# A fused local, downsampled and mixture-of-experts kernel: attention products as 64-row tiles, two heads at once in two PSUM banks

## The chip, the cores and the metric

The kernel runs on one core of a Trainium2 chip. The metric is the device time of one execution in microseconds. Before the change three runs gave 767.11, 763.87 and 763.42 us, so the median is 763.87 us.

## The reference

The inputs q, k and v have 8 batches, 8 heads, 576 positions and 64 elements per head, all fp32. Two attentions are added, and the sum is the token matrix of a mixture of experts.

```python
q_d = q.reshape(B, H, S // 4, 4, D).mean(axis=3)      # k_d, v_d likewise
out_d = sm_attn(q_d, k_d, v_d)                        # 144 x 144 per head
out_up = np.repeat(out_d, 4, axis=2)
mask = np.abs(pos[:, None] - pos[None, :]) < 4        # a band of 7 keys
out_local = softmax(where(mask, q @ k.T / 8, -1e9)) @ v
x = (out_up + out_local) as 4608 tokens of 512
logits = x @ w_gate                                   # 8 experts, 576 tokens each
# tokens and experts are paired greedily by falling logit
out[mask_e] = relu(x[mask_e] @ w1[e]) @ w2[e]
```

## The kernel before, in words

The program has two stages. The first computes the attention, the logits and, while it ends, the first steps of the routing. The second ranks the logits and runs the experts, one after the other, with gathers and scatters of tokens. The change touches the first stage alone.

**Units.** The local attention is cut into windows of 32 queries (QW), 18 of them to a batch; a window needs at most 38 keys (KW). Four windows make a unit `u` of 128 tokens, so there are 36 units, four and a half to a batch. A unit passes the steps s0 and s1 (scores, four heads each), t (the transposed weights), v0 and v1 (products with v), add (the downsampled part is added), st (the token row is stored), lt and lm (transposes and logits).

**Transposed q and k.** `trw` makes Q^T and K^T from rows of the input: four 128x128 transposes on TensorE (PE) fill a PSUM bank, and two copies of 64 partitions by 512 elements take it to SBUF (`evac`, L276 on VectorE (DVE) and L278 on ScalarE (ACT)). There are eight such steps to a batch. `trt` does the last 64 positions by products with the identity matrix (L306). K^T holds two heads, one on partitions 0 to 63 and one on 64 to 127. Q^T is kept in `qz` with a plane for each of the two heads, in which the other head's 64 partitions are zeros, so that a product over all 128 partitions gives one head's scores.

**Local scores and values.** `loc_s` puts the mask into a bank by one product with the identity (L428) and adds 32 products of 32 queries by 38 keys (L436), on four column tiles of the array. DVE takes the maximum and subtracts it (L444, L445), ACT takes the exponential. `loc_t` transposes the weights (L454), and two ACT copies (L465) place them in `pt`, in which zeros separate two windows. `loc_v` does 16 products of 64 columns by 65 (L476); `vw` holds the keys of v of one unit, two windows one above the other on the partitions, with a column of ones for the denominators. `norm` divides (L404, L405, L407).

**Downsampled attention.** `gsum` adds groups of four columns of Q^T and K^T, mostly on GpSimd (POOL). `down_s` makes the scores of three heads in a bank (L325, and L328 for the last 16 positions); DVE reads each bank twice (L331, L333). `down_t` and `down_v` transpose and multiply, and the result goes to DRAM (`up_dram`), from where each unit reads its rows again (`up`).

**PSUM.** All steps of the stage rotate through the eight banks of one pool, `g`.

**Order.** `run` gives every step a time in units (a table of offsets: LOC, TW, DW, DWS, NEXT, LD0, LD1), sorts all steps by it and writes the instructions in that order, with no scheduler behind it. `after(n, f)` puts a step off by n pieces of PE work. All loads of the stage are issued by SyncE (SP) in the same sorted order: `nat` (rows of q, k, v by batch), `natt`, `natw`, and `vw` with four DMAs to a unit.

## Time and profile before

| what | value |
|---|---|
| median of three runs | 763.87 us |
| the profiled execution's own time | 763.21 us |
| its span, first to last instruction | 761.5 us |
| mean granted TensorE clock | 0.948 |
| busy share of the span: PE, DVE, ACT, POOL | 88%, 71%, 44%, 32% |
| weight loads (PEld) | 61% |
| moved by DMA | 126.43 MB, 166 GB/s over the span |
| packets of under 512 bytes | 97012 of 152980 |

The page gives every engine's busy time; the busy share over the whole span mixes the attention stage with the experts, so the stage has to be cut out first. A row of the grouped view names the line, the engine, the tile written and the tiles read, the shape, the number of instructions, their busy time together, the mean of one, and the idle time before them with what ended it. Products of fp32 show two records each, a transpose one. Records of different column tiles overlap in time, so their cost is read from the start of one group to the start of the next and not from the mean of one.

### The profile page before, as it was taken

The page shows a single profiled execution, that of the slowest core. Times are in us where ns is not written, and L with a number is a line of the kernel's source. Part 1 is how long each engine was busy: PE and PEld are TensorE (multiplying, and loading weights), DVE is VectorE, ACT ScalarE, POOL GpSimd, SP SyncE. Part 2 cuts the span into 40 slices and gives each one's busy share as a digit, 9 for nine tenths or more (in the row PEclk, how much of TensorE's full clock was granted, in tenths as well). Part 3 has the DMA queues.
Part 4 walks back from the last instruction along what each step waited for, and adds up shares of the span by engine and source line. Part 5 has one row for each costly group of instructions (what it writes and reads, how often), then busy time and mean ns, then how long its engine had stood idle before and what let it go on. Part 6 is the DMA issues. An engine that isn't in the chain of part 4 may idle for free.

```text
span 761.5 us, 21142 instructions
## 1 busy us (share of the span) xinstructions
PE 673.8 (88%) x8545; PEld 467.4 (61%) x8545; DVE 537.3 (71%) x1614; ACT 333.5 (44%) x646; POOL 245.8 (32%) x282
## 2 busy tenths in 40 slices
PE   7789898898889893399899999999999999999994
PEld 5667676787768772276366457466467475674851
DVE  5977879598786986887879889889888154261200
ACT  3437676475757541341436234326224253342210
POOL 8173544447453751200530613130410402202011
PEclk8979999899999996589999999999999999999998
DMA  9978798998979861530935663684744933404001
GB/s 283 186 189 205 221 205 244 224 261 199 267 209 263 218 195 54 160 124 14 299 98 222 145 220 107 136 273 163 194 163 167 220 109 108 103 2 117 9 28 35
DMA packets 152980, 126.43 MB, mean 166 GB/s; under 512 B 97012, under 2 KB 127220, under 8 KB 152884
## 3 DMA queue, kind: packets, MB, share of 16 engines
q1 hardware_dynamic: 145424, 103.30, 50.7%
q0 software_dynamic: 6512, 21.24, 9.1%
q8 instruction: 68, 1.11, 0.6%
q10 hardware_dynamic: 948, 0.55, 0.3%
q14 instruction: 28, 0.23, 0.1%
HBM read 95.56 MB, written 21.23 MB: 153 GB/s over the span
## 4 chain that ended last, share of the span: by engine, by line
issue 29%; DVE 24%; PE 23%; DMA 12%; POOL 5%; ACT 4%; SPq 1%; POOLq 0%; DVEq 0%; ACTq 0%
PE pX L1139 5%; PE pH L1110 4%; POOL out_dram L1147 3%; DMA up<-up_dram 3%; DVE cmp L709 2%; DMA nat<-in_q_dram 2%; DMA up_dram<-xu 2%; DMA nat<-in_k_dram 2%; PE pR L743 2%; DVE wl L1050 2%; DMA xg<-x_dram,idx 2%; PE g L292 2%; DVE x L407 1%; POOL xg L1074 1%; PE g L476 1%
## 5 line engine op out<-in xcount | busy, mean ns | idle before, releaser
L1110 PE MATMUL pH<-xt,wh 128*128 128x256 f16 (+1 forms) x1024 | 194.2, 287 | 3.3 <-DVE ht L1126 2.5
L1139 PE MATMUL pX<-wh,ht 128*128 128x512 f16 (+1 forms) x640 | 181.3, 382 | 0.0
L1110 PE MATMUL pH<-xt,wl 128*128 128x320 f16 (+1 forms) x512 | 146.4, 286 | 0.0
L1147 POOL DMA_INDIRECT out_dram<-y,idx x40 | 47.8, 1195 | 282.1 <-ACT y L1144 263.1
L1139 PEld LDWEIGHTS <-ht 128*128 128x128 f16 (+1 forms) x960 | 81.1, 100 | 90.1 <-issue 5.6
L1139 PE MATMUL pX<-wl,ht 128*128 128x512 f16 (+1 forms) x320 | 118.9, 382 | 0.0
L1110 PEld LDWEIGHTS <-wh 128*128 128x128 f16 x1024 | 98.0, 98 | 30.7 <-DVE ht L1126 4.2
L1123 ACT ACTIVATE ht<-pH 128x512 f16<-128x512 f32 (+1 forms) x128 | 45.4, 407 | 102.5 <-PE pH L1110 102.4
L1050 DVE SCALAR_TENSOR_TENSOR wl<-nat,wh 128x512 f16<-128x512 f32 x128 | 84.6, 683 | 2.5
L1144 ACT ACTIVATE y<-pX 128x512 f32<-128x512 f32 (+1 forms) x40 | 23.8, 594 | 126.7 <-PE pX L1139 71.1
L1126 DVE SCALAR_TENSOR_TENSOR ht<-pH,ht 128x512 f16<-128x512 f32 (+1 forms) x128 | 52.4, 449 | 34.5 <-ACT ht L1123 34.2
L1074 POOL DMA_INDIRECT xg<-x_dram,idx x40 | 45.0, 1126 | 85.6 <-DVE idx L1001 66.5
L1048 ACT ACTIVATE wh<-nat 128x1024 f16<-128x1024 f32 x64 | 66.9, 1056 | 4.3 <-DMA nat<-in_moe_w_dram 4.2
L465 ACT COPY pt<-g 64x512 f32<-64x512 f32 x72 | 41.7, 579 | 38.0 <-PE g L454 36.8
L1110 PEld LDWEIGHTS <-wl 128*128 128x128 f16 x512 | 50.1, 98 | 12.4 <-issue 0.2
L1094 DVE SCALAR_TENSOR_TENSOR xs<-xg,xs 128x512 f16<-128x512 f32 (+1 forms) x35 | 23.2, 685 | 40.1 <-ACT xs L1093 40.1
L292 PE MATMUL g<-ident,nat 128*128 128x128 f32 x256 | 40.3, 293 | 11.0 <-DMA nat<-in_q_dram 3.6
L476 PE MATMUL g<-vw,pt 128*64 128x65 f32 x1152 | 44.1, 227 | 4.5 <-ACT pt L465 1.8
L476 PEld LDWEIGHTS g<-vw,pt 128*64 128x64 f32 x1152 | 39.1, 140 | 11.5 <-ACT pt L465 6.4
L278 ACT COPY kt<-g 64x512 f32<-64x512 f32 (+1 forms) x53 | 33.3, 629 | 26.0 <-PE g L292 12.0
L265 POOL TENSOR_TENSOR gtmp<-qz 64x576 f32<-64x576 f32 x28 | 32.0, 1142 | 34.0 <-DVE kdt L268 26.2
L499 DVE SCALAR_TENSOR_TENSOR xt<-g,xt 128x512 f16<-128x512 f32 x36 | 24.6, 685 | 21.2 <-ACT xt L498 21.1
(222 smaller groups left out, 1165.8 us busy)
## 6 DMA issues: line engine op xcount, KB each, us to landing
nat<-in_moe_w_dram SPq DMA_DIRECT2D x28, 1024.0 KB
vw<-in_v_dram SPq DMA_DIRECT2D x136, 96.0 KB
up<-up_dram SPq DMA_DIRECT2D x36, 256.0 KB
x_dram<-x SPq DMA_DIRECT2D x36, 256.0 KB
nat<-in_q_dram SPq DMA_DIRECT2D x16, 512.0 KB
nat<-in_k_dram SPq DMA_DIRECT2D x16, 512.0 KB
nat<-in_v_dram SPq DMA_DIRECT2D x14, 512.0 KB
up_dram<-xu SPq DMA_DIRECT2D x16, 128.0 KB
```

Of the source, the lines that this page charges most:

```text
L278: self.nc.scalar.copy(out, in_)
L292: nc.tensor.transpose(p[:, a, :, fp], src[:, 4 * hh + 2 * a + s, 2 * fp:2 * fp + 2].rearrange("p f d -> p (f d)"), self.ident)
L465: self.nc.scalar.copy(out, in_)
L476: nc.tensor.matmul(o[64 * i:64 * i + 64, 65 * h:65 * h + 65], pt[:, 2 * g + i, h].rearrange("p b q -> p (b q)"), self.vw[u % 4][:, i, 4 * ...
L1048: nc.scalar.activation(hi, r, AF.Copy, scale=sc)
L1050: nc.vector.scalar_tensor_tensor(lo[:, a:a + LOP], r[:, a:a + LOP], sc, hi[:, a:a + LOP], op0=OP.mult, op1=OP.subtract)
L1074: self.fetched = nc.gpsimd.indirect_dma_start(out=xg[:n], out_offset=None, in_=self.x, in_offset=bass.IndirectOffsetOnAxis(ap=idx[:n, c:c ...
L1110: mm = nc.tensor.matmul(p[:, s, :s1 - s0], w[d][a][:, 128 * f:128 * f + 128], xt[:, b, d, s0:s1], start=j == 0, stop=j == len(seq) - 1)
L1123: last = nc.scalar.activation(hi, q, AF.Relu)
L1126: nc.vector.scalar_tensor_tensor(lo, q, 0.0, hi, op0=OP.max, op1=OP.subtract)
L1139: nc.tensor.matmul(p[o:o + m], ht[:, f, h0:h0 + m], w[4 + f // 2][b][:, 512 * (f % 2):512 * (f % 2) + 512], start=j < parts, stop=j >= len ...
L1147: i = nc.gpsimd.indirect_dma_start(out=self.out, in_=y[:n], in_offset=None, out_offset=bass.IndirectOffsetOnAxis(ap=idx[:n, c:c + 1], axis=0))
```

## The change

Q^T has no zeros any more: like K^T it holds two heads on 128 partitions. Every product with it names a tile of 64 rows of the array, at row 0 or 64, and the two heads' products follow each other directly. They write two PSUM banks, which are allotted as a pair. The pool has four single banks `g` (NG) and two pairs `gg` (NG2) now; scores of both kinds and the local products with v use pairs, all else single banks.

`trw` makes both heads of a pair at once, by eight products with the identity of 128 rows by 64 columns (L286 in the new program) in place of four transposes, and one copy of 128 partitions by 512. `loc_s` does all eight heads in one step; `loc_t` needs one copy and no zeros; `loc_v` does 32 products of 64 rows by 32 columns in one step, and divides once. `down_s` does six heads in a pair, then two and the last positions. `vw` holds the keys of nine windows, half a sequence, in three buffers, and is loaded by 10 or 12 DMAs whose issue is spread by 0.1 unit. `EV` shares the copies of `evac` evenly between ACT and DVE, where one in five was DVE's; the offsets of the table are other numbers.

```diff
-EV = (0, 0, 0, 0, 1)
+EV = (1, 1, 0, 0)
+NG, NG2 = 4, 2
...
-LD0 = (-2.849, -3.627, -0.654, -0.8, 0.549)
+LD0 = (-2.934, -3.869, -0.654, -0.983, 0.549)
...
-            self.vw.append(cst.tile([128, 2, H, D + 1], F32, name=f"vw{i}"))
+            self.vw.append(cst.tile([128, 9, HP, D + 1], F32, name=f"vw{i}"))
...
+    def bank(self):
+        return self.ps.tile([128, 512], F32, name="g", bufs=NG)
+
+    def banks(self):
+        return self.ps.tile([128, 2, 512], F32, name="gg", bufs=NG2)
...
-    def trw(self, b, which, hh, s):
+    def trw(self, b, which, hp):
...
-        p = self.ps.tile([128, 2, GM, 2], F32, name="g", bufs=8)
-        for a in range(2):
-            for fp in range(2):
-                nc.tensor.transpose(p[:, a, :, fp], src[:, 4 * hh + 2 * a + s, 2 * fp:2 * fp + 2].rearrange("p f d -> p (f d)"),
-                                    self.ident)
...
-        for par in range(2):
-            self.evac(t[:, :, par:4 * GM:2], p[64 * par:64 * par + 64].rearrange("p a i f -> p a (i f)"), par)
+        p = self.bank().rearrange("p (i f) -> p i f", f=4)
+        for f in range(4):
+            for s in range(2):
+                nc.tensor.matmul(p[64 * s:64 * s + 64, :, f], src[:, 2 * hp + s, f], self.ident, start=True, stop=True)
+        self.evac(self.dest(b, which)[:, hp, :4 * GM], p.rearrange("p i f -> p (i f)"))
...
+        def score(o, hp, s):
             r = slice(64 * s, 64 * s + 64)
+            nc.tensor.matmul(o, q[r, hp, :GM], k[r, hp], start=True, stop=True, tile_position=(64 * s, 0))
...
-            for a in range(4):
-                h = 4 * g + a
-                nc.tensor.matmul(sv[32 * a:32 * a + 32, 4 * g + c], self.qz[b % 2][:, h // 2, h % 2, QW * w:QW * w + QW],
-                                 self.kt[b][:, h // 2, key0(w):key0(w) + KW], start=False, stop=True,
-                                 skip_group_check=True, tile_position=(0, 32 * a))
+        for a in range(HP):
+            for c in range(4):
+                b, w = divmod(4 * u + c, NW)
+                for s in range(2):
+                    r = slice(64 * s, 64 * s + 64)
+                    nc.tensor.matmul(o[32 * c:32 * c + 32, s, a], self.xt_["q", b][r, a, QW * w:QW * w + QW],
+                                     self.xt_["k", b][r, a, key0(w):key0(w) + KW], start=False, stop=True,
+                                     skip_group_check=True, tile_position=(64 * s, 32 * c))
...
-        for a in range(2):
-            r = slice(64 * a, 64 * a + 64)
-            self.pevac(a, out[r, :, :, a], p[r].rearrange("p (i h q) -> p i h q", h=4, q=QW))
+        nc.scalar.copy(self.pt[u].rearrange("p a q -> p (a q)"), p)
...
-        for h in range(4):
-            for i in range(2):
-                nc.tensor.matmul(o[64 * i:64 * i + 64, 65 * h:65 * h + 65],
-                                 pt[:, 2 * g + i, h].rearrange("p b q -> p (b q)"),
-                                 self.vw[u % 4][:, i, 4 * g + h], start=True, stop=True)
+        for a in range(HP):
+            for c in range(4):
+                j, i = divmod(4 * u + c, 9)
+                vw = self.vw[j % NVW]
+                for s in range(2):
+                    r = slice(64 * s, 64 * s + 64)
+                    nc.tensor.matmul(o[32 * c:32 * c + 32, s, a], pt[r, a, 32 * c:32 * c + 32], vw[r, i, a],
+                                     start=True, stop=True, tile_position=(64 * s, 32 * c))
```

Two places of the order matter for the prediction. The first is PE about the scores of the downsampled attention, in batch 2. Before, each bank is one of eight; L494 is lt, L476 v, L292 trw, L325 and L328 down_s, L428 and L436 the local scores, L454 t, L306 trt.

```order
L494 MATMUL g<-ident,x 128x128 x4
L476 MATMUL g<-vw_130,pt_134 64x65 x16
L292 MATMUL g<-ident,nat 128x128 x4
L325 MATMUL g<-kdt,qdz_120 128x144 x3
L428 LDWEIGHTS identb
L428 MATMUL g<-mask,identb 128x304
L436 MATMUL g<-kt,qz_119 32x38 x16
L454 MATMUL g<-ident,sw_131 128x128 x4
L436 MATMUL g<-kt,qz_119 32x38 x16
L292 MATMUL g<-ident,nat 128x128 x4
```

In the new program the same work stands like this, `gg` being a pair; L465 is v, L286 trw, L307 and L324 down_s, L426 and L434 the local scores, L450 t.

```order
L465 MATMUL gg<-vw_121,pt 32x65 x32
L286 MATMUL g<-ident,nat 64x128 x16
L307 MATMUL gg<-kdt,qdt 128x144 x6
L426 LDWEIGHTS identb
L426 MATMUL gg<-mask,identb 128x152
L426 LDWEIGHTS identb
L426 MATMUL gg<-mask,identb 128x152
L434 MATMUL gg<-kt,qt 32x38 x32
L450 MATMUL g<-ident,sw_125 128x128 x4
L307 MATMUL gg<-kdt,qdt 128x144 x2
L324 MATMUL gg<-kdt,qdt 32x144 x4
```

v, the first down_s, the local scores and the second down_s now each take one of the two pairs, in this order; t and trw take single banks. The local scores are one step and no longer two with t between them.

The second place is SP at the start, where v's keys are loaded. Before, the first eight `vw` DMAs (units 1 and 0) stand ahead of the last quarter of the next batch's q and k.

```order
L206 DMA natw_162<-in_v_dram 128x1x256
L215 DMA nat_164<-in_v_dram 128x8x256
L215 DMA nat_246<-in_q_dram 128x4x256
L215 DMA nat_248<-in_k_dram 128x4x256
L215 DMA nat_246<-in_q_dram 128x4x256
L229 DMA vw1_128<-in_v_dram 48x8x64 x4
L229 DMA vw0_127<-in_v_dram 48x8x64 x4
L215 DMA nat_248<-in_k_dram 128x4x256
L200 DMA natt_268<-in_q_dram 64x1x256 x2
```

In the new program the pieces of both halves of the sequence alternate; the end of that stretch, after seventeen of their DMAs, reads:

```order
L210 DMA vw1_122<-in_v_dram 48x8x64
L210 DMA vw0_121<-in_v_dram 48x8x64
L183 DMA natt_279<-in_q_dram 64x1x256 x2
L183 DMA natt_279<-in_k_dram 64x1x256 x2
L210 DMA vw1_122<-in_v_dram 48x8x64
L210 DMA vw0_121<-in_v_dram 48x8x64 x2
```

The last pieces of `vw0`, which the first unit's v needs, now stand behind the pieces of `vw1`, behind the whole of the next batch's first q and k and behind its `natt`.

More of the change, by code (lines that the diff above doesn't have):

```diff
@@ L318, in down_s @@
     def down_s(self, b, part):
         nc = self.nc
-        s = self.ps.tile([128, 512], F32, name="g", bufs=8)
-        sv = s[:, :3 * G].rearrange("p (c k) -> p c k", c=3)
-        for c in range(3):
-            hp, i = divmod(3 * part + c, 2)
-            if hp < HP:
-                nc.tensor.matmul(sv[:, c], self.qdz[b % 2][:, hp, i], self.kdt[b][:, hp], start=True, stop=True)
-        if part == 2:
+        q, k = self.xd["q", b], self.xd["k", b]
+        def score(o, hp, s):
+            r = slice(64 * s, 64 * s + 64)
+            nc.tensor.matmul(o, q[r, hp, :GM], k[r, hp], start=True, stop=True, tile_position=(64 * s, 0))
@@ new lines, in down_s @@
+        if part == 0:
+            n = 6
+            o = self.banks()[:, :, :3 * G].rearrange("p s (c k) -> p s c k", c=3)
+            for hp in range(3):
+                for s in range(2):
+                    score(o[:, s, hp], hp, s)
+            t = self.sd[:, :6]
+            tv = t.rearrange("p (c s) k -> p s c k", s=2)
+            todo = (o, tv, 6),
+        else:
+            n = 3
+            o = self.banks()[:, :, :2 * G].rearrange("p s (c k) -> p s c k", c=2)
+            for s in range(2):
+                score(o[:, s, 0], 3, s)
@@ L332, in down_s @@
-        t = self.sd[:, 3 * part:3 * part + 3]
-        nc.vector.tensor_tensor(t, sv, mx[:, :, None].to_broadcast([128, 3, G]), op=OP.subtract)
+            t = self.sd[:, 6:]
+            todo = (o[:, :, 0], t[:, :2], 2), (o[:, 0, 1:], t[:, 2:], 1)
+        for o, tv, m in todo:
+            mx = self.wk.tile([128, m], F32, name=f"mxd{m}")
+            mv = mx.rearrange("p (s c) -> p s c", s=2) if m == 6 else mx
+            nc.vector.tensor_reduce(mv, o, axis=AX.X, op=OP.max)
+            nc.vector.tensor_tensor(tv, o, mv[..., None].to_broadcast(list(o.shape)), op=OP.subtract)
@@ L417, in load_up, with loc_s @@
         self.up[u] = t
-    def loc_s(self, u, g):
+    def loc_s(self, u):
         nc = self.nc
-        if g == 0:
-            s = self.ps.tile([128, 512], F32, name="g", bufs=8)
-            self.so[u] = s
-            nc.tensor.matmul(s[:, :H * KW], self.identb, self.mask[:, None, ukind(u)].to_broadcast([128, 2, 4 * KW]),
+        o = self.banks()[:, :, :HP * KW]
+        for s in range(2):
+            nc.tensor.matmul(o[:, s], self.identb, self.mask[:, None, ukind(u)].to_broadcast([128, HP, KW]),
```

286 lines of the change are left out of this document (129 added, 157 removed).

## The prediction

> **What bounds the kernel now.** I cut the span into stages first, with the busy time of each engine by stretch. The columns are the stretch, its length, then busy time and instructions of PE, weight loads, DVE, ACT and POOL, the granted clock, the busy share of the DMA engines and GB/s.
>
> ```profile
> 0.00:27.00 27.00, 17.95 (x221) 12.75 (x223) 17.16 (x37) 9.55 (x15) 19.78 (x29) 0.87 1.01 262
> 27.00:50.00 23.00, 18.50 (x218) 15.99 (x212) 20.09 (x46) 9.66 (x22) 9.47 (x14) 0.81 0.79 189
> 50.00:150.00 100.00, 88.42 (x1882) 73.72 (x1885) 75.89 (x203) 62.71 (x123) 46.36 (x60) 0.94 0.84 215
> 150.00:245.00 95.00, 85.78 (x1942) 72.56 (x1937) 76.47 (x210) 65.57 (x128) 49.39 (x62) 0.98 0.97 239
> 245.00:289.00 44.00, 37.91 (x935) 31.29 (x921) 39.88 (x122) 22.57 (x46) 24.61 (x33) 1.00 0.75 206
> 289.00:761.00 472.00, 425.21 (x3384) 261.10 (x3384) 307.78 (x1000) 163.40 (x313) 96.20 (x87) 0.95 0.44 131
> ```
>
> The attention ends at about 289 us; nothing later is edited, so the 472 us of the experts stay. Inside the attention three resources are close together: PE is busy 88 to 90% of the two long stretches, DVE 76 to 80%, and the DMA engines 84 and then 97%. ACT (63 to 69%) and POOL (about half) are not close. PE is idle for about 21 us of the 195. The list of waits, from 27 to 289 us, says what ends that idle time (total, times, longest).
>
> ```profile
> PE g L454 <- ACT sw L446: 4.4, 5, 2.1
> PE g L292 <- DMA nat<-in_q_dram: 3.6, 1, 3.6
> PE g L292 <- DMA nat<-in_k_dram: 3.5, 2, 1.8
> PE g L292 <- DVE den L405: 3.2, 1, 3.2
> PE g L370 <- DVE ptd L276: 2.8, 1, 2.8
> PE g L355 <- ACT sd L339: 2.0, 3, 0.9
> PE g L476 <- ACT pt L465: 1.8, 5, 0.7
> ```
>
> About 14 us of it waits for ACT or DVE, 7 us for input rows. So PE work counts nearly in full, and work taken off ACT or POOL counts only through those 14 us.
>
> **The change part by part.** I make the sum against the profiled execution, 763.2 us (span 761.5 and 1.7 around it), which stands 0.7 us under the median of 763.87. Anything within 0.5%, 3.8 us, can't be told from no change.
>
> *Transposes of q and k.* The new form, products with the identity of 64 columns each, stands in the trace already, as the tail's products. PE's instructions in order of time, from 120 to 140 us:
>
> ```profile
> 126.10 1.09 PE L306 MATMUL g<-ident,natt 128*64 128x128 f32 x16
> 127.13 0.55 PE L355 MATMUL g<-ident,sd 128*128 128x128 f32 x3
> ...
> 129.73 0.60 PE L292 MATMUL g<-ident,nat 128*128 128x128 f32 x4
> 130.16 0.29 PE L428 MATMUL g<-mask,identb 128*128 128x304 bf16 x1
> ```
>
> Eight products take 1.03 us from start to next start, the four transposes that make the same amount 0.43 us. There are 64 such steps: 64 x 0.60 = 38 us more on PE. [...]
>
> *Local products.* One unit of the end of the stage, where PE waits for almost nothing:
>
> ```profile
> 268.35 0.30 PE L428 MATMUL g<-mask,identb 128*128 128x304 bf16 x1
> 268.59 0.49 PE L436 MATMUL g<-kt,qz 128*32 128x38 f32 x32
> 269.00 0.66 PE L454 MATMUL g<-ident,sw 128*128 128x128 f32 x4
> 269.59 0.49 PE L436 MATMUL g<-kt,qz 128*32 128x38 f32 x32
> 270.01 0.26 PE L509 MATMUL g<-wg,xt 128*128 128x16 f16 x4
> ...
> 270.99 1.22 PE L476 MATMUL g<-vw,pt 128*64 128x65 f32 x32
> 272.14 0.30 PE L428 MATMUL g<-mask,identb 128*128 128x304 bf16 x1
> ```
>
> Mask, scores and t take 270.01 - 268.35 = 1.66 us. The number of score products stays at 32, but eight tiles of 64 by 32 can be at work where four were. If that halves them, one of the two 0.41 us goes: 1.25 us, 0.4 x 36 = 15 us. v takes 1.15 us on two tiles. The new form has twice the products on eight tiles, so half the time if all eight work together: 0.54 us (with 0.07 us left for the change of tile form) x 36 = 19 us. The trace has no product on fewer than 128 rows, so both gains have a lower end of nothing; above, they can't be more than these halves. I take the halves, since the four column tiles of the scores do work side by side: 32 records in 0.41 us where one record's mean is 202 ns by the row of its group. That row and the others for prices (busy, mean ns, idle before):
>
> ```profile
> L436 PE MATMUL g<-kt,qz 128*32 128x38 f32 x2304 | 35.7, 202 | 2.4 <-DVE kt L276 1.2 <-issue 1.1
> L325 PE MATMUL g<-kdt,qdz 128*128 128x144 f32 x128 | 22.7, 312 | 0.7 <-POOL qdz L268 0.7
> L465 ACT COPY pt<-g 64x512 f32<-64x512 f32 x72 | 41.7, 579 | 38.0 <-PE g L454 36.8
> L278 ACT COPY kt<-g 64x512 f32<-64x512 f32 (+1 forms) x53 | 33.3, 629 | 26.0 <-PE g L292 12.0 <-PE g L306 8.1 <-DVE kt L276 5.3
> L278 ACT COPY qz<-g 64x512 f32<-64x512 f32 (+1 forms) x52 | 32.9, 633 | 14.2 <-PE g L292 12.9 <-DVE qz L276 0.6
> L276 DVE COPY qz<-g 64x512 f32<-64x512 f32 (+1 forms) x28 | 19.1, 684 | 2.9 <-PE g L292 2.4
> L407 DVE TENSOR_TENSOR x<-g,den 128x256 f32<-128x256 f32 x72 | 30.5, 424 | 2.5
> L445 DVE TENSOR_TENSOR sw<-g,mx 128x304 f32<-128x304 f32 x36 | 17.1, 475 | 1.3
> L333 DVE TENSOR_TENSOR sd<-g,mxd 128x432 f32<-128x432 f32 x24 | 14.6, 607 | 0.8
> ```
>
> *Downsampled scores.* 22.7 us of PE, two heads at once: 11 us less, or nothing.
>
> PE together: +38 - 15 - 19 - 11 = **-7 us**, and +38 us where 64-row tiles bring nothing.
>
> *Copies, ACT, DVE, POOL.* The second copy of pt goes: 36 x 0.58 = 21 us of ACT. q and k need one copy of 128 partitions for two of 64, and half of them move to DVE, so ACT's 66 us here fall to about a third, some 45 us less. ACT loses about 65 us of a stage in which it works some 170. DVE gains copies and loses one of two divisions a unit. From L445 to L333 an element costs (607 - 475) / 128 = 1.03 ns, so a division of 512 elements takes 607 + 80 x 1.03 = 690 ns for 2 x 424: 6 us less over 36 units, and one pair of small operations a unit. With the copies I take DVE as unchanged. POOL sums q on 128 partitions at once and drops the zeros; it is covered by its own idle time, half of the stage, so it costs and brings nothing by itself. What lighter ACT and POOL bring comes out of the 14 us of waits above: between 0 and 14, I take **-8 us**.
>
> *PSUM.* Eight banks in turn become four single ones and two pairs. The price is in the waits of PE for a pair, worked out under the rivals: between 0 and 17 us, and I take **+5 us**, about 0.6 a batch, since DVE and ACT catch up in every run of transposes and these have become longer.
>
> *v's keys.* The bytes are the same. At the start SP issues 22 pieces for two half sequences, where 8 stood. Both rows are from the first 30 us, SP's issue and PE's first wait for it:
>
> ```profile
> 12.93 8.32 SPq L229 DMA_DIRECT2D vw<-in_v_dram  x8
> 26.51 1.15 PE L476 MATMUL g<-vw,pt 128*64 128x65 f32 x30 [0.52 <-DMA vw<-in_v_dram]
> ```
>
> A piece takes 1.04 us to issue while the DMA engines are full, so the last piece of the first half lands up to 14 us later than before. PE has work put ahead of that product: the downsampled scores and more transposes, some 7 us at the prices above. Later the keys of units 2 to 4 are there already, which gives DMA time back. Between 0 and 14 us, I take **+5 us**; later in the stage three buffers of nine windows hold more than four of four did, so I see no other wait.
>
> Sum: 763.2 - 7 - 8 + 5 + 5 = 758.2, so **758 us**.
>
> **The rivals.**
>
> *A pair of banks is late (slower).* Between v and the second down_s four steps in a row want one of two pairs. DVE must divide v (0.69 us and two small operations, about 1.0) and then read six heads' scores twice, 864 elements each: 607 + 432 x 1.03 = 1052 ns, so 2.1 us. DVE is behind PE besides: the product v that started at 263.87 us had its last division here.
>
> ```profile
> 263.87 1.15 PE L476 MATMUL g<-vw,pt 128*64 128x65 f32 x32
> ...
> 267.04 0.42 DVE L407 TENSOR_TENSOR x<-g,den 128x256 f32<-128x256 f32 x1
> ```
>
> PE had left the product at about 265.02 (263.87 + 1.15), so the division ended 267.46 - 265.02 = 2.4 us later, of which two halves of 0.42 and four small operations are some 1.5: DVE came 0.9 us late. So the pair of the first down_s comes free 3.1 to 4.0 us after v's end, while PE has to put in between only the six products (about 0.6), the local scores and t (1.25): 1.9 us. PE waits 1.2 to 2.1 us in each batch, 10 to 17 in eight. With the other terms as above it decides from 14 us of such waits on (763.2 - 15 + 5 + 14 = 767.2); with 17, and 10 at the start, the time is 775 us. Against it: only 2.4 pairs are used a unit, and elsewhere transposes stand between. [...]
>
> *64-row tiles do not work side by side.* Then PE has +38 instead of -7, and with the other terms the time is 763 + 38 - 8 + 5 + 5 = 803; if half of the gain is there, 780. Against it, the column tiles. I put its middle at 790 us.
>
> *A wash.* DMA is at 97% from 150 to 245 us and moves the same packets; a faster PE would then only wait for rows of q and k, which already are 7 us of its waits. The middle keeps its length, the end gains a few us, the start loses them: 764 us.
>
> *All waits fall.* If the start is covered, pairs cost nothing and all 14 us go: 763 - 7 - 14 = 742 us. Against it, the seven us that wait for rows stay, and they grow as PE gets there earlier. I take 742 to 751 us.
>
> **How the numbers follow.** My forecast, 758 with its own range of 751 to 759.9, has a chance of 0.31; that all waits fall, 0.11; the wash, 0.25; late pairs, 0.25; tiles that don't work together, 0.08. So faster by over 0.5% is 0.42, within 0.5% 0.25, slower 0.33. The range leaves out the last case and the outer half of the first and of the late pairs: 745 to 778 us.
>
> **What would show it.** In the profile after: eight products L286 at about 1.0 us a step, v at 0.5 to 0.6 us a unit, scores with mask and t at about 1.25; ACT busy some 65 us less; PE's waits for DVE's and ACT's products shorter where they name sw, sd and pt. Waits of PE before L307, L434 or L465 for DVE (mx, mxd, den, the division) would show late pairs, a wait for vw past 30 us the start. A v that still takes about 1.1 us, or a stage's end (the last L501 and L504) later than 289 us, would make the forecast wrong.

## The result, and the profile after

The changed kernel took 800.96 us (median of four runs, 796.43 to 802.89) beside 765.49 us of the kernel before on the same chip: a ratio of 1.045, with an interval of 1.039 to 1.051. Run once more on another chip it came to 792.89 beside 767.99 us, 1.034 (1.025 to 1.043). The change makes the kernel 3.4 to 4.5% slower. The forecast of 758 us and the whole range were too low. All ratios leave out executions more than 1.5% above the fastest of the same kernel, which are few (one of 2296 us in e5) except in e16, where they are five of ten.

These rows of the profile after answer to the first rows shown of before. The page, with the busy time of the engines and the queue that brings instructions (packets, MB, share):

```profile
PE 690.9 (86%) x10501; PEld 478.1 (60%) x10501; DVE 522.7 (65%) x1500; ACT 260.3 (33%) x515; POOL 209.4 (26%) x224
q8 instruction: 82, 1.34, 0.7%
```

The same queue on the page of the kernel before:

```profile
q8 instruction: 68, 1.11, 0.6%
```

The stages of the changed kernel, columns as before:

```profile
0.00:27.00 27.00, 18.65 (x333) 13.95 (x333) 13.57 (x30) 4.72 (x7) 13.33 (x19) 1.00 0.93 254
27.00:50.00 23.00, 17.32 (x351) 14.52 (x351) 12.43 (x28) 5.30 (x13) 4.29 (x5) 0.78 1.03 202
50.00:150.00 100.00, 86.06 (x2386) 70.95 (x2386) 70.53 (x160) 31.98 (x68) 36.03 (x42) 0.95 0.81 214
150.00:245.00 95.00, 81.72 (x2323) 67.10 (x2321) 69.93 (x162) 30.45 (x64) 33.12 (x38) 0.93 0.84 219
245.00:314.00 69.00, 58.80 (x1737) 49.38 (x1733) 46.95 (x123) 24.09 (x51) 27.08 (x32) 0.90 0.58 161
314.00:800.00 486.00, 428.36 (x3386) 262.24 (x3384) 309.27 (x1000) 163.77 (x314) 95.57 (x89) 0.94 0.43 127
```

The attention ends at 314 us where it ended at 288. In the attention ACT is busy 97 us where it was busy 170, DVE and DMA less, and PE is still busy 85 to 86% of the long stretches: everything that was to be relieved is relieved, and the stage is longer. The last row is 14 us longer too, though nothing is edited there.

The page also follows the chain of work that ended last and gives each engine's share of the span. Before:

```profile
issue 29%; DVE 24%; PE 23%; DMA 12%; POOL 5%; ACT 4%; SPq 1%; POOLq 0%; DVEq 0%; ACTq 0%
```

and after:

```profile
PE 36%; issue 30%; DVE 17%; DMA 6%; POOL 4%; ACT 4%; SPq 2%; POOLq 0%; ACTq 0%; DVEq 0%
```

Followed through the attention alone, the chain before was PE for 26% of the time, DVE for 31% and DMA for 27%. After the change it is PE for 60% (54% when the kernel was run again, e6). So before the change PE was busy nearly all the time, and yet the work that ended last ran through PE for only a quarter of it.

PE's waits from 27 to 314 us (total, times, longest):

```profile
PE gg L465 <- issue: 10.2, 6, 2.3
PE g L296 <- DMA natt<-in_k_dram: 5.6, 1, 5.6
PE gg L426 <- DVE x L470: 3.7, 4, 2.1
PE gg L307 <- DVE qdt L247: 3.2, 1, 3.2
PE gg L324 <- issue: 2.4, 1, 2.4
PE gg L434 <- issue: 2.4, 4, 0.9
PE g L286 <- issue: 2.4, 2, 1.7
PE g L354 <- ACT sd L338: 2.3, 5, 1.0
```

The waits for products of ACT and DVE have shrunk. In their place stands "issue", a wait for nothing that the profile shows, above all inside v (L465).

### What a wait called "issue" is here

PE's timeline around the two longest of those in v, in the changed kernel (start, length, what, with the idle time before a row in brackets):

```profile
83.48 0.45 PE L465 MATMUL gg<-vw,pt 64*32 64x65 f32 x28 [0.23 <-DVE lg L506]
86.08 0.88 PE L465 MATMUL gg<-vw,pt 64*32 64x65 f32 x36 [2.15 <-issue]
86.89 0.43 PE L426 MATMUL gg<-mask,identb 128*128 128x152 bf16 x2
87.25 0.93 PE L434 MATMUL gg<-kt,qt 64*32 64x38 f32 x64
88.12 1.11 PE L450 MATMUL g<-ident,sw 128*128 128x128 f32 x4
89.02 0.72 PE L486 MATMUL g<-ident,x 128*128 128x128 f32 x4
89.58 0.25 PE L501 MATMUL g<-wg,xt 128*128 128x16 f16 x4
89.68 0.24 PE L504 MATMUL g<-wg,xt 128*128 128x8 f16 x4
89.96 0.32 PE L465 MATMUL gg<-vw,pt 64*32 64x65 f32 x9
92.62 0.68 PE L465 MATMUL gg<-vw,pt 64*32 64x65 f32 x32 [2.35 <-issue]
```

Both waits stand in the middle of one step's like products, whose operands were all there. Each record of a product counts as one instruction of PE here (an fp32 product has two), and each has a weight load. From the one wait to the other PE works off 36 + 2 + 64 + 4 x 4 + 9 = 127 product records, as many weight loads, and two semaphore instructions: 256. And in the whole trace 2 x 10501 such instructions and 145 others came in 82 packets, 258 a packet, 16 KB each. So PE's program comes in blocks of 256 instructions. I counted all of PE's records in the trace: 19 waits of over 0.3 us in the attention stand exactly at such a block's end, 22.9 us together; in the kernel before, three with 3.4 us. A block's packet starts 1.8 us (median) after the first instruction of the block before it, takes 1.15 us (median), and in all 19 waits PE went on 1.2 to 1.7 us after it had landed: some 4.5 us. That is a middle value and no sharp limit: of the blocks that PE worked off in under 4.5 us, 11 of 20 ended in such a wait, of the longer ones 8 of 35. From one block's start to the next it took less than 4 us in two of 40 cases in the kernel before and in nine of 55 in the changed one, where the shortest took 2.5.

### The profile page after: what moved, and what is told of

It is laid out like the page before. It is cut to its first block, busy times and chain, and to the rows that moved or that the text cites. A ratio compares the mean times of both kernels' runs of the same rounds, so it can differ in the third digit from the quotient of the medians.

```text
span 800.3 us, 24625 instructions
## 1 busy us (share of the span) xinstructions
PE 690.9 (86%) x10501; PEld 478.1 (60%) x10501; DVE 522.7 (65%) x1500; ACT 260.3 (33%) x515; POOL 209.4 (26%) x224
## 4 chain that ended last, share of the span: by engine, by line
PE 36%; issue 30%; DVE 17%; DMA 6%; POOL 4%; ACT 4%; SPq 2%; POOLq 0%; ACTq 0%; DVEq 0%
PE g L286 7%; PE pH L1098 4%; PE pX L1127 4%; PE gg L465 3%; POOL out_dram L1135 3%; DMA xg<-x_dram,idx 2%; DVE cmp L697 2%; PE g L450 2%; PE gg L434 2%; PE g L372 2%; PE pR L731 2%; POOL xg L1062 2%; PE g L486 1%; PE g L354 1%; DVE wl L1038 1%
## 5 line engine op out<-in xcount | busy, mean ns | idle before, releaser
L1127 PEld LDWEIGHTS <-ht 128*128 128x128 f16 (+1 forms) x960 | 81.8, 101 | 93.3 <-issue 9.9
L1114 DVE SCALAR_TENSOR_TENSOR ht<-pH,ht 128x512 f16<-128x512 f32 (+1 forms) x128 | 52.4, 450 | 33.8 <-ACT ht L1111 33.5
L286 PE MATMUL g<-ident,nat 128*64 128x128 f32 x1024 | 70.5, 285 | 3.1 <-issue 2.4
L286 PEld LDWEIGHTS g<-ident,nat 128*64 128x64 f32 x1024 | 58.0, 141 | 11.0 <-issue 6.0
L1098 PEld LDWEIGHTS <-wl 128*128 128x128 f16 x512 | 50.3, 98 | 12.7 <-issue 0.2
L452 ACT COPY pt<-g 128x512 f32<-128x512 f32 x36 | 21.1, 585 | 90.2 <-PE g L450 90.2
L465 PE MATMUL gg<-vw,pt 64*32 64x65 f32 x2304 | 34.6, 236 | 14.8 <-issue 10.2
L465 PEld LDWEIGHTS gg<-vw,pt 64*32 64x32 f32 x2304 | 27.2, 111 | 19.4 <-issue 12.6
L246 POOL TENSOR_TENSOR gtmp<-kt 128x576 f32<-128x576 f32 x7 | 8.0, 1146 | 107.4 <-DVE kt L259 71.4
L731 PEld LDWEIGHTS <-cmp 128*128 128x128 bf16 x504 | 16.7, 97 | 30.8 <-DVE cmp L697 19.3
```

What stands on the lines that cost most here:

```text
L286: nc.tensor.matmul(p[64 * s:64 * s + 64, :, f], src[:, 2 * hp + s, f], self.ident, start=True, stop=True)
L465: nc.tensor.matmul(o[32 * c:32 * c + 32, s, a], pt[r, a, 32 * c:32 * c + 32], vw[r, i, a], start=True, stop=True, tile_position=(64 * s, 3 ...
L731: nc.tensor.matmul(cv[:m * J, :, :m], cmp[:, t:t + m].rearrange("p t j -> p (t j)"), oh[:, :, t:t + m], start=t == 0, stop=t + m == NT, sk ...
L1098: mm = nc.tensor.matmul(p[:, s, :s1 - s0], w[d][a][:, 128 * f:128 * f + 128], xt[:, b, d, s0:s1], start=j == 0, stop=j == len(seq) - 1)
L1114: nc.vector.scalar_tensor_tensor(lo, q, 0.0, hi, op0=OP.max, op1=OP.subtract)
L1127: nc.tensor.matmul(p[o:o + m], ht[:, f, h0:h0 + m], w[4 + f // 2][b][:, 512 * (f % 2):512 * (f % 2) + 512], start=j < parts, stop=j >= len ...
```

## The experiments

For every kernel the same account was drawn up from its trace. PE's work is the time from a product's start to the next, at most the product's own duration; where the clock's records say half speed, half of it counts as work and half as lost to the clock; the rest is waits. Ratio and interval are against the kernel before on the same chip, the other columns one profiled execution, in us. Work, clock and waits add up to the attention's length by their making, so the account shows where time went and not by itself why. The two executions of the changed kernel (changed and e6) differ by 3 us in the attention and 5 in the experts; differences of that size in one row say nothing. "Experts" is from their first product with the weights to the last, "at block ends" the part of the waits that stands at a block's end.

| kernel | ratio (interval) | attention ends | PE's work | lost to clock | PE's waits | at block ends | experts |
|---|---|---|---|---|---|---|---|
| before | 1 | 288.3 | 233.8 | 14.6 | 38.7 | 3.4 | 427.0 |
| changed | 1.045 (1.039-1.051) | 313.9 | 242.7 | 19.7 | 50.2 | 22.9 | 440.6 |
| e6 changed, again | 1.034 (1.025-1.043) | 310.6 | 244.9 | 15.6 | 48.9 | 21.8 | 435.2 |
| e1 old transposes | 1.041 (1.033-1.049) | 310.7 | 206.5 | 34.4 | 68.6 | 24.4 | 430.3 |
| e2 keys' order | 1.033 (1.025-1.041) | 310.0 | 240.5 | 27.5 | 40.8 | 20.8 | 432.3 |
| e3 three pairs | 1.064 (1.054-1.073) | 330.3 | 251.1 | 12.7 | 65.3 | 17.3 | 430.7 |
| e8 old v | 1.029 (1.021-1.036) | 309.3 | 255.0 | 8.9 | 44.1 | 7.3 | 437.1 |
| e9 old v, old transposes | 1.032 (1.025-1.040) | 301.9 | 225.4 | 10.6 | 64.7 | 4.5 | 435.4 |
| e13 as e9, one pair | 1.045 (1.037-1.053) | 322.9 | 215.4 | 39.2 | 67.1 | 2.1 | 436.1 |
| e12 old offsets | 1.043 (1.032-1.054) | 316.4 | 245.4 | 19.0 | 50.8 | 21.0 | 432.3 |
| e18 eight banks in turn | 1.039 (1.033-1.044) | 312.7 | 245.3 | 18.4 | 47.8 | 30.2 | 429.2 |
| e19 as e18, old transposes | 1.034 (1.028-1.040) | 306.4 | 208.4 | 32.2 | 64.5 | 27.5 | 429.9 |
| e5 before, products for transposes | 1.008 (1.004-1.012) | 290.1 | 268.6 | 0.1 | 20.3 | 6.3 | 427.4 |
| e17 as e5, two batches | 1.006 (1.002-1.010) | 290.0 | 242.4 | 11.0 | 35.5 | 3.2 | 427.1 |
| e7 before, v split | 1.010 (1.003-1.018) | 295.4 | 239.1 | 11.7 | 43.4 | 23.9 | 432.0 |
| e10 before, six banks | 1.007 (1.003-1.012) | 284.1 | 235.6 | 13.3 | 33.9 | 2.5 | 429.3 |
| e11 before, new offsets | 1.016 (1.007-1.025) | 286.2 | 236.6 | 6.1 | 42.3 | 2.5 | 433.5 |
| e14 before, new local scores | 1.044 (1.036-1.053) | 307.6 | 234.9 | 13.1 | 58.4 | 2.7 | 428.3 |
| e15 before, new downsampled scores | 1.024 (1.016-1.032) | 299.3 | 237.6 | 8.8 | 51.6 | 1.6 | 425.5 |
| e16 as e14, six banks and one pair | 1.003 (0.998-1.008) | 287.0 | 229.1 | 9.2 | 47.5 | 6.6 | 434.0 |

The profile of e16 is of a long execution, 773 us where the shortest took 755; over all ten executions its median is 1.010 times that of the kernel before.

### First round: which part is it?

Three theories: A, the products in place of transposes fill PE; B, the waits for pairs of banks and for v's keys; C, the supply of instructions, read from "issue" alone. The blocks were not counted yet.

**e1**, the old transposes and their copies in the changed kernel.

```diff
-                nc.tensor.matmul(p[64 * s:64 * s + 64, :, f], src[:, 2 * hp + s, f], self.ident, start=True, stop=True)
+                nc.tensor.transpose(p[:, a, :, fp], src[:, 4 * hh + 2 * a + s, 2 * fp:2 * fp + 2]..., self.ident)
```

> The changed kernel, but q and k are transposed as before: four 128x128 transposes a step, two copies of 64 partitions, one copy step in five on VectorE. All else stays as changed. Theory A (the products with the identity fill PE): PE's work falls by some 33 us of the 64 steps and the time by 25 to 35 us from about 801, to 766 to 776 us. Theory B (PE waits for bank pairs and for v's keys at the start): these waits stay, and the time stays above 790 us. Theory C (PE runs out of instructions, waits that name only issue): 1500 fewer PE instructions of 21000 take away a part of about 20 us, 790 to 797 us.

It took 791.18 us, 1.041, not told apart from the changed kernel. A fell: PE's work went down by 36 to 38 us, and the time stayed. The account shows where it went: 15 to 19 us to the clock and 18 to 20 to waits. The time lies in B's range and in C's, but C's gain is not seen: with 1500 instructions fewer the waits at block ends are 24.4 us.

**e2**, the keys of the first two half sequences loaded apart.

```diff
-LD0 = (-2.934, -3.869, -0.654, -0.983, 0.549)
+LD0 = (-2.934, -3.869, -1.9, 0.6, 0.549)
```

> The changed kernel with two numbers of the load table altered, so that the first half sequence of v's keys is loaded ahead of the next batch's q and k, and the second half after them. Theory B (the start): the first product with v starts at about 28 instead of 38 us and the end comes 6 to 10 us earlier, 791 to 795 us. Theory A: the first product comes earlier too, but by the third unit the changed kernel had already caught up with the kernel before, so the time stays within 3 us of 801.

788.41 us, 1.033 (1.025 to 1.041): the interval overlaps those of both measurements of the changed kernel, so nothing is shown to be won. The first product with v starts at 33.0 us where it started at 38.3, and the attention ends at 310.0 us, e6's at 310.6.

**e3**, two single banks and three pairs.

```diff
-NG, NG2 = 4, 2
+NG, NG2 = 2, 3
```

> The changed kernel with three pairs of banks and two single banks instead of two pairs and four. Theory B (pairs are late): PE's waits before the local scores, the downsampled scores and v go, some 8 to 10 us: 791 to 794 us, unless two single banks are too few. Theory A: no gain; with two single banks for transposes and all else PE waits there, 801 to 820 us.

810.08 us, 1.064: more pairs at the cost of single banks lose 1.8 to 2.9%. PE's waits before L307, L426 and L465 for DVE's reading of pairs, 7.7 us in the changed kernel, are gone, and waits for single banks have come instead. So it shows that two single banks are too few, and not what a third pair would bring by itself.

**e5**, the kernel before with the new products in place of its transposes, all else as it was.

```diff
-                nc.tensor.transpose(p[:, a, :, fp], src[...], self.ident)
+                for par in range(2):
+                    nc.tensor.matmul(p[64 * par:64 * par + 64, a, :, fp], src[:, 4 * hh + 2 * a + s, 2 * fp + par],
+                                     self.ident, start=True, stop=True)
```

> The kernel before with one part of the change alone: each of its 128x128 transposes of q and k is made by two products with the identity of 64 columns, into the same place; copies and all else stay. Theory A: 64 steps cost about 0.5 us more each on PE, so 25 to 33 us more, 788 to 797 us. Theory B: nothing about pairs or keys changes, so within 5 us of 764. Theory C: as many more PE instructions as the changed transposes have, some 6 more pieces of 16 KB to fetch: 768 to 776 us.

766.23 us, 1.008, within 5 us of 764 as theory B had it and 6 us over the kernel before on the same chip. PE got 35 us more work and the attention became 2 us longer. From 30 to 150 us the stage looks like this in the kernel before:

```profile
30.00:150.00 120.00, 104.03 (x2069) 87.20 (x2070) 93.26 (x243) 71.91 (x144) 55.83 (x73) 0.92 0.84 213
```

in e5:

```profile
30.00:150.00 120.00, 115.16 (x2524) 95.46 (x2521) 98.36 (x255) 74.22 (x148) 61.10 (x79) 1.00 0.91 225
```

and in e1:

```profile
30.00:150.00 120.00, 93.27 (x2304) 76.96 (x2305) 80.25 (x176) 53.34 (x108) 38.11 (x44) 0.80 0.80 208
```

The granted clock is 0.92, 1.00 and 0.80, and PE is busy 104.0, 115.2 and 93.3 us of these 120: of the three, the one with more to do had the faster clock. In the records of the kernel before and of the changed one every stretch of one clock but the last is a whole number of steps of 3.41 us, at full clock or at half. In these two executions all 17 steps at full clock in which PE was busy less than 0.44 of the time were followed by a halved one, 5 of the 23 between 0.47 and 0.70, and none of the 360 above that. So the 36 us that e1 takes off PE come back, one half as waits (18 to 20 us) and the other as a slower clock (15 to 19 us).

### Second round: blocks or other waits?

F: the waits at block ends make the loss. W: waits for engines, banks and loads make it, and the blocks are chance.

**e6**, the changed kernel again.

> The changed kernel once more, nothing edited. In its first profile 25.5 us were lost in the attention and 13.6 us in the experts, whose code is the same. If the loss in the experts belongs to the change, they take about 440 us again and the time is 4.5% above the kernel before, 792 to 798 us where that takes 760. If it was a matter of one execution, they take 427 to 433 us, as in the three relatives of this kernel, and the time is 785 to 790.

Between the two cases: experts 435.2 us, time 1.034. The experts' loss is not steady; it is not explained by the attention's length either (e1: 430.3).

**e7**, the kernel before with each product of v made as two of 32 columns.

```diff
+                for c in range(2):
-                nc.tensor.matmul(o[64 * i:64 * i + 64, ...], pt[:, 2 * g + i, h].rearrange("p b q -> p (b q)"), ...)
+                    nc.tensor.matmul(o[64 * i + 32 * c:64 * i + 32 * c + 32, ...], pt[:, 2 * g + i, h, c], ...,
+                                     tile_position=(0, 64 * i + 32 * c))
```

> The kernel before, in which each product with v of 64 columns is made as two of 32 columns on tiles of their own: the same sums, 2304 instructions more on PE (those that the change adds in v), nothing else. Theory F (PE's instructions come in blocks of 256, and a block that is worked off in less than about 4 us leaves PE waiting for the next one): waits at the block ends rise from 3 us to 8 to 18 us, and the time is 766 to 776 us where the kernel before takes 760. Theory W (the loss is made of waits for other engines, for pairs of banks and for loads, and the blocks are chance): v takes no longer, and the time is within 4 us of 760.

777.91 us, 1.010 (1.003 to 1.018). The waits at block ends rose from 3.4 to 23.9 us, more than F had it, and the time is within F's range. PE's list of waits in e7 is headed by the two rows that the kernel before does not have at this size:

```profile
PE g L477 <- issue: 13.0, 13, 3.8
PE g L436 <- issue: 8.9, 8, 2.5
```

So many short products one behind the other make these waits; that much is shown. But 20.5 us of them made the attention only 7 us longer: all waits together rose by 5, because the other waits, for DVE, ACT and the loads, fell from 35 to 20.

**e8**, t, v and the loads of the keys as before, in the changed kernel (four single banks, two pairs).

```diff
-PEL = ("s", "t", "v", "lt", "lm")
+PEL = ("s", "t", "v0", "v1", "lt", "lm")
-                    nc.tensor.matmul(o[32 * c:32 * c + 32, s, a], pt[r, a, 32 * c:32 * c + 32], vw[r, i, a],
+                nc.tensor.matmul(o[64 * i:64 * i + 64, 65 * h:65 * h + 65], pt[:, 2 * g + i, h].rearrange("p b q -> p (b q)"),
+                                 self.vw[u % 4][:, i, 2 * h + g], start=True, stop=True)
```

> The changed kernel with t, v and the loads of v's keys as before (products of 64 columns on 128 rows, two copies with zeros between, keys by unit, two single banks); scores, transposes and copies of q and k stay changed. PE has about 11 us more to do and 2304 instructions fewer, ACT 21 us more of copies. Theory F: the waits at block ends fall from 23 us to under 8, and the attention, 314 us in the changed kernel, ends at 295 to 302 us; time 772 to 785. Theory W: the waits stay, in part under other names, 15 us or more of them at block ends, and the time is 795 or more.

791.26 us, 1.029. Block ends 7.3 us as F expected, PE's work 10 us up as expected, the clock better by 7, and yet the attention ends at 309.3. Other waits have come:

```profile
PE gg L306 <- DVE sd L331: 7.9, 6, 2.2
PE g L464 <- ACT pt L453: 7.4, 11, 0.8
PE gg L306 <- DVE qdt L246: 4.0, 2, 3.1
```

Pairs that DVE still reads (L306 is the first downsampled score), and products with v that wait for ACT. F's end and time failed, and so did W, which had the block ends at 15 us or more and the time at 795 or more.

**e9**, as e8 with the old transposes, e1's edit.

> As the one before, with the old transposes of q and k as well: of the change only the scores on 64 rows, Q^T without zeros, the copies to it and the table of offsets are left. PE has about 25 us less to do than the changed kernel, with 3840 instructions fewer. Theory F: waits at block ends under 8 us; PE is busy less, so its clock is granted in half more often than in the changed kernel; time 760 to 772. Theory W: above 780. By my old sum for what is left (PE -20, copies -8, pairs +5) it would be 740 us.

791.22 us, 1.032. 20 us of work and 17 us of block ends are gone against e6, and the attention still ends at 301.9, with 64.7 us of waits, 60 of them away from block ends. The time is above 780, as W had it, and the old sum's 740 is far off. F also had the clock halved more often, since PE has less to do; 10.6 us were lost to the clock where it was 15.6 in e6, so that is not shown. After e8 and e9 neither theory alone does it.

### Third round: banks or order?

P: too few banks. T: the table of offsets.

**e10**, the kernel before with six banks in turn.

```diff
-        p = self.ps.tile([128, 2, GM, 2], F32, name="g", bufs=8)
+        p = self.ps.tile([128, 2, GM, 2], F32, name="g", bufs=6)
```

> The kernel before with six banks of PSUM in turn in place of eight, nothing else. Theory P (the change leaves too few banks: a local score takes two for one, the downsampled scores four for three, and the rest turn in four): PE waits for banks that DVE and ACT still read, 8 to 20 us more in the attention, time 1.0 to 2.6% above the kernel before. If the eight banks are not used up, within 0.4%.

1.007 (1.003 to 1.012), between the two forecasts; in its profile the attention is not longer (284.1).

**e11**, the new numbers of NEXT, TW, DW, DWS, LOC, LD0, LD1 and the rest in the kernel before; **e12**, the old numbers in the changed kernel. Of e11's lines for instance:

```diff
-TW = (0.129, 2.439)
-DW = (-0.791, 2.251)
+TW = (0.129, 2.554)
+DW = (-0.768, 2.251)
```

> The kernel before with the offsets of the changed one (when transposes, downsampled steps, loads, additions, logits come), all code as before. Theory T (the order, not the new forms, costs the time): 1 to 2.6% above the kernel before. If the order is not the cause, within 0.5%.

> The changed kernel with the offsets of the kernel before, all code as changed (keys by half sequences, their first two loads where the old ones stood). Theory T: 1 to 2.6% faster than the changed kernel, that is 1.012 to 1.03 of the kernel before. If the order is not the cause, within 0.5% of the changed kernel (1.035 to 1.045) or slower, since the new numbers were made for the new steps.

e11: 1.016 (1.007 to 1.025), within T's range, but not in the attention (286.2); the experts take 6.5 us longer. e12: 1.043, no faster than the changed kernel; but there v waits 9.9 us for its keys, which it doesn't do with the new numbers. So e11 shows that the new order alone does not lengthen the attention of the kernel before; what it does in the changed kernel e12 doesn't tell cleanly.

**e13**, e9 with another split.

```diff
-NG, NG2 = 4, 2
+NG, NG2 = 6, 1
```

> The kernel with scores on 64 rows alone (e9), with six single banks and one pair in place of four and two. In e9 PE waited some 17 us for single banks that ACT's copies of pt or DVE's divisions held, and 9 us for a pair that the downsampled scores held. Theory P: the waits for single banks fall under 6 us, those for the pair rise by 5 to 10; the attention, 302 us in e9, ends between 292 and 300. If single banks are not short: 302 or later.

800.79 us, 1.045; the attention ends at 322.9, the opposite of P's forecast. With one pair the local scores wait for DVE's reading of the downsampled ones (up to 300 us):

```profile
PE gg L429 <- DVE sd L335: 21.7, 8, 4.4
```

### Fourth round: one part alone

**e14**, the local scores alone on 64 rows, in a pair, in the kernel before; **e15**, the downsampled scores alone; both with four single banks and two pairs. **e16** is e14 with six and one. All take Q^T from the 64 rows of `qz` that are not zeros.

```diff
-                nc.tensor.matmul(sv[32 * a:32 * a + 32, 4 * g + c], self.qz[b % 2][:, h // 2, h % 2, QW * w:QW * w + QW],
+                    nc.tensor.matmul(o[32 * a:32 * a + 32, s, c], self.qz[b % 2][r, a, s, QW * w:QW * w + QW],
```

> The kernel before in which the local scores alone are made on 64 rows, two heads at once in a pair of banks, in one step of eight heads; four single banks and two pairs; Q^T keeps its zeros, all else as before. Theory R (the new scores with their pairs are the root): 1.5 to 3% slower. Theory S (every part costs a little, none much): within 0.8%. By the terms of my old sum it would be 5 us faster.

> The kernel before in which the downsampled scores alone are made on 64 rows in pairs, six heads and then two with the last positions; four single banks and two pairs, all else as before. PE has 5 to 10 us less to do, DVE reads six heads in two long steps. Theory R: 1.5 to 3% slower, with waits of PE for the pair that DVE reads. Theory S: within 0.8%. By my old sum 7 to 11 us faster.

> As the kernel with the local scores alone (e14), with six single banks and one pair. One pair serves one score a unit, and DVE has read it long before the next. If single banks were short in e14, this one is 0.5 to 1% faster than e14; if not, within 0.4% of it. It may come out up to 0.6% under the kernel before, since PE saves some 5 us of scores.

e14: 1.044, as much as the whole change. e16: 1.003 (0.998 to 1.008), with the same products. So in the kernel before it is the split into four single banks and two pairs that costs, not the new scores. PE's waits in e14 (up to 290 us) are mostly for single banks and for steps that ACT is late with:

```profile
PE g L359 <- ACT qz L279: 5.2, 4, 1.8
PE g L476 <- ACT pt L465: 4.9, 9, 0.8
PE g L310 <- DMA natt<-in_k_dram: 3.6, 1, 3.6
PE g L296 <- ACT pt L465: 3.0, 3, 1.3
PE g L494 <- DVE den L408: 2.8, 5, 1.0
```

e15: 1.024, within R's range. Six banks in one pool (e10) cost at most 1.2%; four for all that is not a score cost 2.4 and 4.4%.

**e17**, e5's products for the first two batches alone.

```diff
+                if b > 1:
+                    nc.tensor.transpose(p[:, a, :, fp], src[...], self.ident)
+                    continue
                 for par in range(2):
```

> The kernel before with products in place of transposes for the first two batches alone, some 10 us more of PE work in the first 75 us. With products in all batches PE's clock was never halved and the attention was 3 to 4 us ahead at the eighth unit. If the clock is what pays there, the clock is not halved before 75 us, the attention ends 2 to 4 us earlier and the time is 0.2 to 0.6% under the kernel before; if the work counts, it is 0.5 to 1.3% over it.

1.006 (1.002 to 1.010), the lower edge of what was expected if work counts; the clock was still halved for 27 us of the attention. Nothing is won there.

### Last round: the changed kernel without the split of its banks

B: the split is the root, here too. I: instruction blocks and PE's work are.

**e18**, a pair is two banks of one pool of eight; DVE reads each by itself.

```diff
-        return self.ps.tile([128, 2, 512], F32, name="gg", bufs=NG2)
+        return [self.bank() for _ in range(2)]
```

> The changed kernel with eight banks in turn as before: a pair is two banks of the one pool, so that DVE reads each bank by itself (one more maximum, subtraction, sum and division a unit, some 0.3 us of DVE each 8 us). Theory B (the split of the banks is the root): the attention, 311 to 314 us in the changed kernel, ends at 293 to 302, the time is 1.005 to 1.025 of the kernel before; waits at block ends stay near 20 us, since the instructions are the same. Theory I (the instruction blocks and PE's work are the root): 1.03 to 1.045 as it is.

787.81 us, 1.039, as theory I had it. PE's list of waits up to 305 us has next to none for banks any more:

```profile
PE g L466 <- issue: 16.0, 11, 2.7
PE g L296 <- DMA natt<-in_k_dram: 6.6, 2, 5.6
PE g L434 <- issue: 4.4, 7, 1.7
PE g L451 <- issue: 3.3, 1, 3.3
PE g L307 <- issue: 2.9, 2, 2.5
```

and the attention ends at 312.7 as before: the block ends have grown to 30.2 us. In the changed kernel, then, undoing the split wins nothing, though the split costs in e14. (DVE has one maximum, subtraction, sum and division a unit more to do in e18. Two divisions of 256 elements took 2 x 424 ns in the kernel before and one of 512 takes 691 ns in the changed one, so the division alone is, as an estimate from these, 0.16 us more a unit; that may hide a small gain.)

**e19**, e18 with the old transposes.

> As e18, with the old transposes of q and k (four in place of eight products, two copies of 64 partitions), 38 us less for PE. With four and two banks this step gave nothing that can be told (1.041 against 1.034 to 1.045). Theory B: PE's work counts again in part, 0.99 to 1.012 of the kernel before. Theory I: no faster than e18, and waits at block ends of 20 us or more.

784.41 us, 1.034. All four executions (780.78 to 785.34 us) are shorter than all four of e18 (787.5 to 789.21) on the same chip, by 0.4%, so 37 us less work of PE are worth 3 us here. Block ends are at 27.5 us, 32.2 are lost to the clock. B fell here too, and of theory I the part "no faster than e18" just misses. No version came out faster than the kernel before.

## Why the prediction was wrong, point by point

Two steps of the sum failed. The gain of the local and downsampled products from 64-row tiles was taken as a full halving, 45 us, and measured 24, so that PE got 9 us more work and not 7 less. And the sum had nothing for the supply of PE's instructions, which took 19 us more of waits. Besides, the rule by which the terms were added, that PE work counts nearly in full, does not hold in this kernel. Of the prediction's own signs of being wrong the later end of the stage came true; v did get shorter, but not by half.

**What bounds the kernel.** "PE work counts nearly in full" was wrong both ways. 35 us more of it cost 2 us of the attention (e5), 36 us less brought at most 3 (e1). Waits and clock took up the rest: in e5 waits were 20.3 us for 38.7 and the loss to the clock 0.1 for 14.6, in e1 waits were 18 to 20 us more and the loss to the clock 15 to 19 more than in the changed kernel. A busy share of 88% hid that; PE's 26% of the chain that ended last shows it, in the trace of before already, and in e5, with the 35 us more, PE has 62% of that chain.

**Transposes.** 64 steps at 1.03 us: one stands at 152.73 to 153.76 in the changed kernel. +33 us of PE's work measured, +38 forecast. Nearly right as a term; by e5 it is worth 2 us of the attention and 0.8% of the time.

**Local scores and v.** One unit of the changed kernel at full clock:

```profile
153.76 0.31 PE L426 MATMUL gg<-mask,identb 128*128 128x152 bf16 x2
153.99 0.77 PE L434 MATMUL gg<-kt,qt 64*32 64x38 f32 x64
154.70 0.66 PE L450 MATMUL g<-ident,sw 128*128 128x128 f32 x4
155.19 0.60 PE L486 MATMUL g<-ident,x 128*128 128x128 f32 x4
...
156.03 0.86 PE L465 MATMUL gg<-vw,pt 64*32 64x65 f32 x64
156.82 0.31 PE L426 MATMUL gg<-mask,identb 128*128 128x152 bf16 x2
```

Mask, scores and t take 1.43 us, v 0.79, where I put 1.25 and 0.5 to 0.6. Here is the step of the sum that failed: "I take the halves, since the four column tiles of the scores do work side by side: 32 records in 0.41 us". 0.41 us for 32 records is 12.8 ns each, and the new scores take 0.71 us for 64, 11.1 ns; the new v 0.79 for 64, 12.3 ns. So the scores have as many records as before, and twice the tiles took only an eighth off the spacing. v gained, with twice the records, because its 32 had come every 36 ns (1.15 us). In e7, with v's 64 records on four tiles of 128 rows, they come 16.5 ns apart (median of the undisturbed steps), so there the eight tiles are worth a quarter and not a half. Why the spacing doesn't halve is open: inside a step records start 6 to 7 ns apart in runs of four to 32 and then pause or come more slowly (in the L434 above a pause of 71 ns follows the 32nd record), so 11 to 13 ns is a mean and not shown to be a floor. All units together: scores and t 6 us less for 15, v 11 for 19, downsampled scores 7 for 11.

**PE together:** 33 - 6 - 11 - 7 = +9 us, by the account of the whole stage +9 to +11, where the sum had -7. Of my rivals, the tiles that bring half of their gain, at 780 us, had the direction; I gave it and its neighbour 0.08.

**The term that was not in the sum** is the supply of instructions: 1956 more product records and as many weight loads, in dense runs, and 19 us more of waits at block ends. The row of L436 in the prediction even ends in "<-issue 1.1", and the list of waits from 27 to 289 us, of which the prediction shows seven rows, goes on with

```profile
PE g L306 <- issue: 1.7, 1, 1.7
PE g L436 <- issue: 1.1, 1, 1.1
```

I did not ask what that was. (The prediction also sets that list beside the 21 us of idle time between 50 and 245 us; from 27 to 289 us PE is idle for some 31.)

**Lighter ACT, pairs of banks, the start.** Forecast -8, +5 and +5. The waits outside block ends fell from 35 to 27 us, so the three together are -8 for +2. ACT's busy time fell by 74 us, where 65 were forecast, and DVE's division of 512 elements took 691 ns where I had worked out 690. The pairs cost about what I put (waits for x, sd and denl before L307, L426 and L465 are 7.7 us), yet taking them away gives no time (e18), so the rival of the late pairs is not the cause. At the start the first v came 12.6 us later, but not for want of its keys: PE has no wait for vw in the changed kernel, and waited 5.6 us for the natt rows of k instead. By the second unit's t, 52.4 us for 52.2, nothing of the delay was left: 0, the lower end of my range.

**The sum as measured:** +9 of work, +19 at block ends, +5 of clock, -8 of other waits: 25 us, and the attention ends 25.6 later, as it must by this account. 13.6 us more were lost in the experts in this execution, 8.2 in e6. Here the forecast said that the experts stay; over all kernels they took 425.5 to 440.6 us, and what moves them isn't settled.

**What stays open.** That dense runs of short products make waits at block ends is shown (by the count, and by e7). That these waits alone make the loss is not: e8 took them away and put waits for banks in their place, and a kernel with the old v and eight banks in turn was not run. The terms don't add up singly either: five parts undone, one at a time, each left a ratio of 1.029 to 1.043 (e1, e2, e8, e12, e18). What fits all of it, and is argued and not shown, is that DVE, ACT and the loads stand close behind PE, so that whatever one part gives, another takes. What moves the experts by up to 15 us is open too.

## What to carry to other kernels

Count instructions, not only their time: where short products follow each other closely, divide PE's instructions by the blocks they come in (256 here), and ask whether a block lasts as long as the next one takes to arrive (some 4.5 us here, as a middle value). Before halving a step because more tiles are at work, divide its time by its records; where that was already near the shortest mean spacing in the trace, eight tiles for four took an eighth off it here (scores, 12.8 to 11.1 ns) or a quarter (v, 16.5 to 12.3 ns), and not a half. Look at the chain that ended last, and not only at busy shares, before calling an engine the limit. And where PE waits a little everywhere, test its price by adding work before building anything that removes some: e5 was a change of three lines and showed that 35 us of work were worth 2 us of the attention.

## What the runs showed of the hardware that was not expected

- Records of fp32 products on tiles of 32 columns start 11 to 17 ns apart in the mean of a step: scores at 12.8 on four tiles of 128 rows and 11.1 on eight of 64, v at 16.5 (e7) and 12.3. Inside a step they come 6 to 7 ns apart, with pauses.
- PE's instructions came in packets of 16 KB for 256 of them (82 packets for 21147 instructions in the changed kernel), one block ahead: a packet started 1.8 us (median) after the first instruction of the block before it. Of the blocks worked off in under 4.5 us about half (11 of 20 in the changed kernel) ended in a wait; the longest wait was 3.8 us (e7).
- The clock's records went in steps of 3.41 us in the kernel before and the changed one. A step at full clock with PE busy less than 0.44 of the time was followed by a halved one in 17 of 17 cases, one between 0.47 and 0.70 in 5 of 23, one above that in none of 360. With 35 us more work (e5) the clock wasn't halved once before 289 us, with 36 us less (e1) it was for 78 us.
